# First scores on all 128 rows, with zero-padded copies of the queries, and no idle matmuls in the middle

## The chip, the core and the metric

The kernel runs on one core of a Trainium2 chip. The metric is the device time of one execution in microseconds (us); of several runs the median counts. The engines are PE (TensorE: matmuls, with PEld for its weight loads), DVE (VectorE), ACT (ScalarE), POOL (GpSimd) and SP (SyncE, which here issues DMAs). SBUF has 128 partitions. PSUM has 8 banks of 128 x 512 fp32; matmuls write there.

## The reference

Two attention layers over 2048 tokens of width 512, with 32 heads of 16, side by side in the output.

```python
def _A_ref(x, wqkv, wo):
    qkv = (x @ wqkv).reshape(B, S, 3, H, Dh).transpose(2, 0, 3, 1, 4)
    q, k, v = qkv[0], qkv[1], qkv[2]
    scores = jnp.einsum("bhqd,bhkd->bhqk", q, k) * Dh ** -0.5
    p = _softmax(scores, axis=-1)
    o = jnp.einsum("bhqk,bhkd->bhqd", p, v)
    return o.transpose(0, 2, 1, 3).reshape(B, S, D) @ wo

def _B_ref(x, wqkv, w_phi, wo):
    ...
    pq = jnp.einsum("bhsd,hdf->bhsf", q, w_phi)
    pk = jnp.einsum("bhsd,hdf->bhsf", k, w_phi)
    phi_q = concatenate([softmax(pq), softmax(-pq)], -1)
    phi_k = concatenate([softmax(pk), softmax(-pk)], -1)
    kv = jnp.einsum("bhsf,bhsd->bhfd", phi_k, v)
    z = jnp.einsum("bhsf->bhf", phi_k)
    num = jnp.einsum("bhqf,bhfd->bhqd", phi_q, kv)
    den = jnp.einsum("bhqf,bhf->bhq", phi_q, z)[..., None] + 1e-6
    return (num / den).transpose(0, 2, 1, 3).reshape(B, S, D) @ wo

return jnp.concatenate([a, b], axis=-1)
```

Layer A, full softmax attention, is nearly all of the work. Layer B, linear attention, runs in the gaps.

## The kernel before

Layer A is cut into 32 units. A unit is a group of four heads (`g`, eight groups) and a chunk of 512 queries (`c`, four chunks). Four heads of 16 are laid out at partitions 0, 32, 64 and 96: head r of a group has its 16 rows at 32r, followed by 16 rows which in the queries' tile are zero at first. `QT` holds the projected queries that way, `KT` the keys, whose rows 16 and 17 of each block are ones.

Each unit has two phases. In the first one the scores are computed with the queries as stationary operand (`emit_m1`, L716 to L728): 128 queries x 512 keys for one head per matmul, each on 32 rows of the array, at the tile position of its head. Two heads at a time fill two PSUM banks (0 and 1, or 2 and 3, alternately), and DVE takes the maximum over the keys (`emit_r1`, L735). After 32 such steps `emit_mchain` (L744 to L756) writes the negative maxima, in two bf16 parts, into rows 16 and 17 of the query blocks, by way of POOL, a DMA transpose and two DMAs. In the second phase (`emit_m2`, L771) the scores are computed again, transposed: 128 keys x 512 queries for one head, now with the maximum subtracted, since the keys' rows 16 and 17 are ones. ACT takes the exponential into one of the `RING` slots of `pT` (L782), and `emit_pv` (L796) multiplies it by the values plus a column of ones, four heads at a time, each on 17 columns of the array, all into bank 7. Banks 4, 5 and 6 go round among the second scores and the background pieces.

The order of work on each engine is written out by a planner: one loop over slots `tau`. In slot `tau` PE gets the two first-score matmuls of step `tau`, the two second-score matmuls of step `tau - LAG` (43 slots behind), every second slot the four matmuls of `emit_pv`, and then one background piece (`bg_step`) if one is due. Such a piece is mostly four full matmuls: projections of layer A (L321, L333), work of layer B (L452, L528, L634), the output projection (L661). If the slot has fewer than `NCOL = 2` columns of work after the scores, `emit_fill` (L823) adds idle matmuls: groups of four, each on 17 columns, a tile of ones times a tile of zeros, into bank 7, where they add zero. DVE gets the maximum of the slot, ACT the two exponentials and the copies out of PSUM.

PE executes in order. A first-score matmul of step `tau` waits for DVE's maximum of step `tau - 2`, which read the same banks. A second score waits until ACT has read the bank it takes.

Unit 0 takes its steps in another order than the rest, so that it can begin with the first keys. `u` counts units and `NQ` = 32 is the slots of a unit; the 1024 steps of first scores are followed by 46 slots in which the second phase runs out, and then by the last unit's end (`emit_last`).

SP issues its DMAs in order and waits in order as well: in a unit's course the copy of the sums out of `X` (`lr`, L834), their reciprocals to `Yd` (L846), four copies that spread these over 16 rows each (L849), and the two DMAs of the maxima for the second phase. POOL multiplies (L859) once the L849 copies have landed.

Layer B's feature maps use `uB` and `eB`, both double, one piece every 26 slots.

Of the kernel before, what the change touches and what calls it, by code (L numbers as in the profile page):

```python
# [94 lines left out]
def bass_concat_heads__softmax_full_mha__linear_kernel_hedgehog__prompt_kernel(  # L95
# [11 lines left out]
    NQ = 8 * NKC  # L107
    NB = 4 * NKT
    NU = NG * NQC
    RING = 16  # L110
    LAGX = 11
    PVLAG = 3
    RMLAG = 1
    NCOL = 2
# [3 lines left out]
    units = [(g, c) for c in range(NQC) for g in range(NG)]  # L118

    with contextlib.ExitStack() as es:  # L120
        block = es.enter_context(nc.Block())

        def sb(name, shape, dt):
            return es.enter_context(nc.sbuf_tensor(name, shape, dt))

        P = _Plan()
# [14 lines left out]
        PS = es.enter_context(nc.psum_tensor("PS", [128, 8, 512], F32))  # L141
# [13 lines left out]
        WKp = sb("WKp", [128, 4, NG, 128], BF)  # L155
        WOp = sb("WOp", [128, NG, 512], BF)
        QT = sb("QT", [128, NG, S], BF)
        KT = sb("KT", [128, NG, S], BF)
        VP = sb("VP", [128, NKT, H, 17], BF)
        pT = sb("pT", [128, RING, 512], BF)  # L160
        X = sb("X", [128, 2, 512], F32)
# [7 lines left out]
        woB = sb("woB", [128, 4, 512], BF)  # L169
        qmask = sb("qmask", [128, 4], F32)  # L170
        pB = sb("pB", [128, 2, 512], F32)
        uB = sb("uB", [128, 2, 1024], F32)
        eB = sb("eB", [128, 2, 1024], BF)
        sB = sb("sB", [128, 512], F32)
        mB = sb("mB", [128, 2, 2, 32], F32)
# [59 lines left out]
        t_stage0 = P.op("pool", lambda e: e.memset(flat(stage).bitcast(U32), 0), [t_wkp])  # L235
        t_bd0 = P.op("pool", lambda e: e.memset(flat(BD).bitcast(U32), 0))
        t_wo0 = P.op("pool", lambda e: e.memset(flat(WOp).bitcast(U32), 0))
        t_vp1 = P.op("pool", lambda e: e.memset(VP[:, :, :, 16:17], 1.0))
        t_yd1 = P.op("pool", lambda e: e.memset(Yd[:], 1.0))
        t_vb1 = P.op("pool", lambda e: e.memset(vB[:], 1.0))  # L240
# [23 lines left out]
        def later(slot, fn):  # L264
            calls.setdefault(slot, []).append(fn)
# [47 lines left out]
        qt_ready = {}  # L313
        kt_ready = {}
# [98 lines left out]
        users = {}  # L413

        def use(key):
            return users.get(key, [])
# [21 lines left out]
        def fm(n):  # L438
            x, st = (1, n) if n < NKT else (0, n - NKT)
            i = n % 2  # L440
            cx = {}
# [5 lines left out]
            def p_fin(b, tok, tau):  # L447
# [9 lines left out]
            u4 = uB[:, i, :].rearrange("p (h s f) -> p h s f", s=2, f=16)  # L457
# [10 lines left out]
            def sub(tau):  # L468
                def mb(k):
                    return mB[:, i, k, :].unsqueeze(2).broadcast_to([128, H, 16])  # L470
                P.op("pool", lambda e: e.tensor_tensor(u4[:, :, 0, :], p3, mb(0), ALU.subtract),  # L471
                     [cx["mx"]] + use(("u", i)))
                cx["u"] = P.op("pool", lambda e: e.tensor_tensor(u4[:, :, 1, :], mb(1), p3, ALU.subtract), [cx["mn"]])
                users[("p", i)] = [cx["u"]]
                users[("m", i)] = [cx["u"]]
                later(tau + 5, lambda: ex(tau + 5))

            def ex(tau):
                cx["e"] = P.op("act", lambda e: e.activation(eB[:, i, :], uB[:, i, :], ACT.Exp),  # L479
                               [cx["u"]] + use(("e", i)))  # L480
                users[("u", i)] = [cx["e"]]
                s = pool_slot(tau + 2)
                later(s, lambda: sums(s))

# [161 lines left out]
        for n in range(2 * NKT):  # L646
            fm(n)
# [28 lines left out]
        d_sh = [dsem("sh0"), dsem("sh1")]  # L676
        d_mt = [dsem("mt0"), dsem("mt1")]
        d_mr = [dsem("mr0"), dsem("mr1")]
        PVB = PS[:, 7, :]

        r1 = {}
# [18 lines left out]
        total_q1 = NU * NQ  # L700
# [14 lines left out]
        def emit_m1(q1):  # L715
            u, qt, kc, half = decode_q1(q1)  # L716
            g, c = units[u]
            q0 = c * 512 + qt * 128
            deps = [qt_ready[(g, c)], kt_ready[(g, kc)], r1.get(q1 - 2)]
            tok = None  # L720
            for i in range(2):
                r = 2 * half + i
                tok = P.op("pe", lambda e, r=r: e.matmul(  # L723
                    PS[:, r, :], QT[32 * r:32 * r + 32, g, q0:q0 + 128],
                    KT[32 * r:32 * r + 32, g, kc * 512:(kc + 1) * 512],
                    start=True, stop=True, tile_position=(32 * r, 0)), deps, signal=(i == 1))
                deps = []
            m1[q1] = tok  # L728

        def emit_r1(q1):  # L730
            u, qt, kc, half = decode_q1(q1)
# [47 lines left out]
        def emit_exp(B):  # L779
            slot = B % RING  # L780
            bank = bank_of[B]
# [5 lines left out]
        def emit_pv(u, kt):  # L787
# [6 lines left out]
            for B in Bs:  # L794
                r = block_info(B)[2]
                tok = P.op("pe", lambda e, B=B, r=r: e.matmul(  # L796
                    PVB[32 * r:32 * r + 17, :], VP[:, kt, 4 * g + r, :], pT[:, B % RING, :],
                    start=(kt == 0), stop=(kt == NKT - 1), tile_position=(0, 32 * r)),
# [9 lines left out]
            for B in Bs:  # L808
                slot_reader[B % RING] = tok
            pv_t[(u, kt)] = tok  # L810
# [68 lines left out]
        def emit_last():  # L879
# [21 lines left out]
            for k in range(4):  # L901
# [8 lines left out]
                else:  # L910
                    t = P.op("dve", lambda e, k=k, bank=bank: e.tensor_copy(ou[:, k, :], PS[:, bank, :]), deps)
                P.dma("sp" if k % 2 == 0 else "act", d_last[k], lambda e, st=st, k=k: e.dma_start(
                    out[0][st * 128:(st + 1) * 128, 0:512], ou[:, k, :]), [t])

        tau = 0
        while tau <= max(pv_in_slot) or jobs or running or calls:
            if tau < total_q1:
                emit_m1(tau)
            Pg = tau - LAG
            blocks = [2 * Pg, 2 * Pg + 1] if 0 <= Pg < total_q1 else []  # L920
            for B in blocks:
                emit_m2(B)
            for B in blocks:
                emit_exp(B)
            for fn in calls.pop(tau, []):
                fn()
            ncol = 0
            for (u, kt) in pv_in_slot.get(tau, []):
                emit_pv(u, kt)
                ncol += 1  # L930
                if u == NU - 1:
                    ncol += 1
                if kt == NKT - 1 and u == NU - 1:
# [69 lines left out]
```

## Time and profile before

| | us |
|---|---|
| median of 3 runs | 1341.0 |
| lowest, highest | 1339.66, 1344.04 |
| span of the profiled execution | 3156.6 |
| PE busy in it | 3152.2 |
| DVE busy in it | 1304.1 |
| ACT busy in it | 1296.2 |
| POOL busy in it | 307.0 |

The span of the profiled execution, from its first to its last instruction, is longer than the timed runs by more than a factor of two. No time is given for the profiled execution beside its span.

A row of a group reads: line, engine, operation, output<-inputs, shape, number | busy us, mean ns of one | idle time of the engine just before them and what ended it. A row of the timeline reads: start, duration, engine, line, operation. The ends of matmuls are modelled, so intervals between starts say more than durations. In a row of the stretches come the window, its length, and then busy time and number for PE, PEld, DVE, ACT and POOL, the granted clock of PE, and the share and rate of the DMAs.

### The profile page before, as it was taken

What the parts mean: (1) busy time and instruction counts of PE and PEld (TensorE: products, weight loads), DVE (VectorE), ACT (ScalarE), POOL (GpSimd) and SP (SyncE); (2) the same over time, 40 slices, a digit from 0 to 9 for tenths busy, and PEclk for the clock granted to TensorE, in tenths of its full rate; (3) what the DMA queues carried; (4) which work ended last, traced back from release to release, by engine and by line L of the source; (5) the groups of instructions that cost most, each with busy time, mean ns of one, the idle gap of its engine ahead of it and who ended that gap; (6) DMA issues with size and microseconds to landing.
All of it is one profiled execution on the core that took longest, in us unless ns stands there. A gap on an engine that the chain in (4) does not pass through costs nothing.

```text
span 3156.6 us, 29062 instructions
## 1 busy us (share of the span) xinstructions
PE 3152.2 (100%) x12226; PEld 362.2 (11%) x12226; DVE 1304.1 (41%) x1130; ACT 1296.2 (41%) x2479; POOL 307.0 (10%) x423
## 2 busy tenths in 40 slices
PE   9999999999999999999999999999999999999999
PEld 1111001111111111110011111111111111111111
DVE  1222223444444544544454435444454444445410
ACT  0001223444444444444444435444444444444442
POOL 1000000000011111111111101111111111111100
DMA  2000001000000000000000000000000000100000
GB/s 53 0 0 24 0 11 18 8 2 3 2 2 3 3 6 6 3 3 3 3 3 3 3 8 7 11 11 10 13 10 11 10 16 11 13 10 10 11 5 7
DMA packets 68939, 26.66 MB, mean 8 GB/s; under 512 B 59656, under 2 KB 66824, under 8 KB 68808
## 3 DMA queue, kind: packets, MB, share of 16 engines
q1 hardware_dynamic: 67464, 23.49, 5.4%
q8 instruction: 96, 1.57, 0.2%
q10 hardware_dynamic: 1344, 1.31, 0.1%
q14 instruction: 35, 0.29, 0.0%
HBM read 3.16 MB, written 4.19 MB: 2 GB/s over the span
## 4 chain that ended last, share of the span: by engine, by line
PE 99%; issue 0%; ACT 0%; POOL 0%; DVE 0%; POOLq 0%
PE PS L823 35%; PE PS L723 28%; PE PS L796 11%; PE PS L333 8%; PE PS L452 3%; PE PS L321 3%; PE PS L661 3%; PE PS L528 2%; PE PS L634 2%; PE PS L771 2%; PE PS L369 1%; PE PS L874 1%; PE PS L804 1%; PE PS L589 0%; PE PS L541 0%
## 5 line engine op out<-in xcount | busy, mean ns | idle before, releaser
L735 DVE TENSOR_REDUCE part<-PS 128x2 f32<-128x1024 f32 x1024 | 1255.2, 1226 | 1676.9 <-PE PS L723 1007.5
L782 ACT ACTIVATE pT<-PS 128x512 bf16<-128x512 f32 x2048 | 1111.5, 594 | 1262.1 <-PE PS L771 663.9
L823 PE MATMUL PS<-zmv,ones_t 128*17 128x512 bf16 x5004 | 1217.8, 973 | 0.3 <-ACT pT L782 0.3
L723 PE MATMUL PS<-KT,QT 32*128 32x512 bf16 x2048 | 959.5, 931 | 0.8 <-DVE QT L341 0.8
L771 PE MATMUL PS<-QT,KT 32*128 32x512 bf16 x2048 | 932.2, 902 | 0.0
L796 PE MATMUL PS<-pT,VP 128*17 128x512 bf16 x2048 | 457.2, 782 | 0.0
L723 PEld LDWEIGHTS PS<-KT,QT 32*128 32x128 bf16 x2048 | 111.0, 101 | 1580.8 <-DVE part L735 1102.9
L333 PE MATMUL PS<-xAT,WKp 128*128 128x512 bf16 x128 | 151.8, 1446 | 0.0
L823 PEld LDWEIGHTS PS<-zmv,ones_t 128*17 128x17 bf16 x5004 | 88.9, 88 | 315.1 <-issue 298.6
L771 PEld LDWEIGHTS PS<-QT,KT 32*128 32x128 bf16 x2048 | 111.1, 101 | 64.9 <-ACT pT L782 51.5
L333 PE MATMUL PS<-xAT,WQp 128*128 128x512 bf16 x128 | 116.5, 1122 | 0.0
L748 POOL TENSOR_SCALAR stage<-mrow 128x16 bf16<-128x16 f32 x32 | 8.1, 253 | 1070.4 <-DVE mrow L744 1070.4
L452 PE MATMUL PS<-WKp,xBT 128*128 128x512 bf16 x128 | 106.8, 1051 | 0.0
L345 ACT ACTIVATE KT<-PS,bias_k 128x512 bf16<-128x512 f32 x32 | 22.0, 687 | 194.9 <-PE PS L333 194.9
L507 POOL TENSOR_TENSOR wA<-eB,rB 128x1024 bf16<-128x1024 bf16 x32 | 61.7, 1929 | 398.1 <-ACT rB L501 398.1
L796 PEld LDWEIGHTS PS<-pT,VP 128*17 128x17 bf16 x2048 | 49.6, 87 | 378.0 <-issue 356.3
L321 PE MATMUL PS<-wA,xAT 128*128 128x512 bf16 x64 | 84.3, 1598 | 0.0
L859 POOL TENSOR_TENSOR QT<-X,Yd 128x256 bf16<-128x256 f32 x62 | 43.6, 725 | 400.6 <-DMA Yd<-Yd 400.4
L661 PE MATMUL PS<-WOp,QT 128*128 128x512 bf16 x96 | 80.8, 1063 | 0.0
L486 POOL TENSOR_TENSOR sB<-eB 128x512 f32<-128x512 bf16 x32 | 36.9, 1154 | 374.5 <-ACT eB L479 374.5
L471 POOL TENSOR_TENSOR uB<-pB,mB 128x512 f32<-128x512 f32 x32 | 33.9, 1058 | 395.9 <-DVE mB L462 395.9
L309 ACT ACTIVATE QT<-PS 128x512 bf16<-128x512 f32 x31 | 18.5, 597 | 93.7 <-PE PS L333 93.7
(78 smaller groups left out, 713.8 us busy)
## 6 DMA issues: line engine op xcount, KB each, us to landing
Yd<-Yd SPq DMA_DIRECT2D x124, 32.0 KB, 3.2
out_dram<-xAT SPq DMA_DIRECT2D x16, 128.0 KB, 1.7
out_dram<-OA SPq DMA_DIRECT2D x12, 128.0 KB, 1.7
wA<-in_A_wqkv_dram ACTq DMA_DIRECT2D x2, 512.0 KB, 5.0
QT<-mcols SPq DMA_DIRECT2D x64, 4.0 KB
wA<-in_A_wqkv_dram SPq DMA_DIRECT2D x1, 512.0 KB, 4.3
WOp<-in_A_wo_dram SPq DMA_DIRECT2D x4, 128.0 KB, 4.4
BD<-in_B_w_phi_dram SPq DMA_DIRECT2D x32, 0.5 KB, 1.6
```

The source lines that it names most:

```text
L321: piece = mm_piece(4, lambda e, b, ct: e.matmul(PS[:, b, :], xAT[:, ct, kt * 128:(kt + 1) * 128], wA[:, ct, 1024:1536], start=(ct == 0), s ...
L333: piece = mm_piece(4, lambda e, b, ct: e.matmul(PS[:, b, :], wpad[:, ct, g, :], xAT[:, ct, c * 512:(c + 1) * 512], start=(ct == 0), stop=( ...
L452: add_job(slot, [mm_piece(4, lambda e, b, ct: e.matmul(PS[:, b, :], xBT[:, ct, st * 128:(st + 1) * 128], Wf[:, x, ct, :], start=(ct == 0), ...
L528: piece = mm_piece(4, lambda e, b, ct: e.matmul(PS[:, b, :], xBT[:, ct, st * 128:(st + 1) * 128], wA[:, ct, 0:512], start=(ct == 0), stop= ...
L634: piece = mm_piece(4, lambda e, b, t: e.matmul(PS[:, b, :], oTB[:, i, t, :], woB[:, t, :], start=(t == 0), stop=(t == 3)), lambda: [cx["ot ...
L661: return mm_piece(4, lambda e, b, i: e.matmul(PS[:, b, :], QT[:, 4 * p + i, st * 128:(st + 1) * 128], WOp[:, 4 * p + i, :], start=(p == 0 ...
L723: tok = P.op("pe", lambda e, r=r: e.matmul(PS[:, r, :], QT[32 * r:32 * r + 32, g, q0:q0 + 128], KT[32 * r:32 * r + 32, g, kc * 512:(kc + 1 ...
L735: r1[q1] = P.op("dve", lambda e: e.tensor_reduce(part[:, u % 2, 2 * half:2 * half + 2, qt, kc], PS[:, 2 * half:2 * half + 2, :], AX.X, ALU ...
L771: m2_t[B] = P.op("pe", lambda e: e.matmul(PS[:, bank, :], KT[32 * r:32 * r + 32, g, kt * 128:(kt + 1) * 128], QT[32 * r:32 * r + 32, g, c ...
L782: exp_t[B] = P.op("act", lambda e: e.activation(pT[:, slot, :], PS[:, bank, :], ACT.Exp, scale=0.25), [m2_t[B], slot_reader.get(slot)])
L796: tok = P.op("pe", lambda e, B=B, r=r: e.matmul(PVB[32 * r:32 * r + 17, :], VP[:, kt, 4 * g + r, :], pT[:, B % RING, :], start=(kt == 0), ...
L823: P.op("pe", lambda e, cq=cq: e.matmul(PS[32 * cq:32 * cq + 17, bank, :], ones_t[:, 0:17], zmv[:, :], start=(bank != 7), stop=(bank != 7), ...
```

## The change

Five things are changed.

- A new tile `Q4` holds, for two units in turn, four copies of a unit's queries: copy r has the 16 rows of head r and zeros in all others. POOL zeroes it once at the start; four DMAs on SP (`emit_q4`) fill the 16 rows of each copy, 14 slots ahead of the unit (8 ahead of unit 1).
- From unit 1 on, a first score is one matmul on all 128 rows: stationary operand 128 queries out of `Q4`, moving operand 512 keys with all four heads. The zeros take the other heads out. Unit 0 keeps its form.
- `emit_fill` is called only in the first 32 slots and in the slots after the last first score.
- `RING`, the number of slots for exponentials, goes from 16 to 12.
- `uB` goes from two buffers to one.

```diff
-    RING = 16
+    RING = 12
...
+        Q4 = sb("Q4", [128, 2, 4, 512], BF)
...
-        uB = sb("uB", [128, 2, 1024], F32)
+        uB = sb("uB", [128, 1, 1024], F32)
...
         t_wo0 = P.op("pool", lambda e: e.memset(flat(WOp).bitcast(U32), 0))
+        t_q40 = P.op("pool", lambda e: e.memset(Q4[:].rearrange("p a b c -> p (a b c)").bitcast(U32), 0))
...
+        d_q4 = [dsem("q40"), dsem("q41")]
+        q4_t = {}
+        last_m1 = {}
+
+        def emit_q4(u):
+            g, c = units[u]
+            ub = u % 2
+            for r in range(4):
+                q4_t[u] = P.dma("sp", d_q4[ub], lambda e, r=r: e.dma_start(
+                    Q4[32 * r:32 * r + 16, ub, r, :], QT[32 * r:32 * r + 16, g, c * 512:(c + 1) * 512]),
+                    [qt_ready[(g, c)], t_q40, last_m1.get(u - 2)])
...
-            deps = [qt_ready[(g, c)], kt_ready[(g, kc)], r1.get(q1 - 2)]
+            deps = [kt_ready[(g, kc)], r1.get(q1 - 2)] + [qt_ready[(g, c)] if u == 0 else q4_t[u]]
...
-                tok = P.op("pe", lambda e, r=r: e.matmul(
-                    PS[:, r, :], QT[32 * r:32 * r + 32, g, q0:q0 + 128],
-                    KT[32 * r:32 * r + 32, g, kc * 512:(kc + 1) * 512],
-                    start=True, stop=True, tile_position=(32 * r, 0)), deps, signal=(i == 1))
+                if u == 0:
+                    tok = P.op("pe", lambda e, r=r: e.matmul(
+                        PS[:, r, :], QT[32 * r:32 * r + 32, g, q0:q0 + 128],
+                        KT[32 * r:32 * r + 32, g, kc * 512:(kc + 1) * 512],
+                        start=True, stop=True, tile_position=(32 * r, 0)), deps, signal=(i == 1))
+                else:
+                    tok = P.op("pe", lambda e, r=r: e.matmul(
+                        PS[:, r, :], Q4[:, u % 2, r, qt * 128:(qt + 1) * 128],
+                        KT[:, g, kc * 512:(kc + 1) * 512], start=True, stop=True), deps, signal=(i == 1))
                 deps = []
             m1[q1] = tok
+            last_m1[u] = tok
...
+        for u in range(1, NU):
+            later(u * NQ - 14 if u > 1 else NQ - 8, lambda u=u: emit_q4(u))
...
-            if ncol < NCOL:
+            if ncol < (NCOL if tau < NQ or tau >= total_q1 else 0):
                 emit_fill(NCOL - ncol)
```

In the changed file the first scores from unit 1 on stand at L742, the second scores at L790, the idle matmuls at L842, the copies at L689.

More of the change, by code (lines that the diff above doesn't have):

```diff
@@ L456, in fm @@
             p3 = pB[:, i, :].rearrange("p (h f) -> p h f", f=16)
-            u4 = uB[:, i, :].rearrange("p (h s f) -> p h s f", s=2, f=16)
+            u4 = uB[:, 0, :].rearrange("p (h s f) -> p h s f", s=2, f=16)
             e3 = eB[:, i, :].rearrange("p (g f) -> p g f", f=16)
@@ L471, in sub @@
                 P.op("pool", lambda e: e.tensor_tensor(u4[:, :, 0, :], p3, mb(0), ALU.subtract),
-                     [cx["mx"]] + use(("u", i)))
+                     [cx["mx"]] + use(("u", 0)))
                 cx["u"] = P.op("pool", lambda e: e.tensor_tensor(u4[:, :, 1, :], mb(1), p3, ALU.subtract), [cx["mn"]])
@@ L478, in ex @@
             def ex(tau):
-                cx["e"] = P.op("act", lambda e: e.activation(eB[:, i, :], uB[:, i, :], ACT.Exp),
+                cx["e"] = P.op("act", lambda e: e.activation(eB[:, i, :], uB[:, 0, :], ACT.Exp),
                                [cx["u"]] + use(("e", i)))
-                users[("u", i)] = [cx["e"]]
+                users[("u", 0)] = [cx["e"]]
                 s = pool_slot(tau + 2)
```

## The prediction

> **What bounds the kernel now.** I read the page's head and busy shares first, then the costliest groups, the stretches before and after 490 us, and last the timeline of single slots. A slot is one turn of the planner's loop: two first-score matmuls with one maximum on DVE, and two second-score matmuls with two exponentials on ACT.
>
> ```profile
> span 3156.6 us, 29062 instructions
> PE 3152.2 (100%) x12226; PEld 362.2 (11%) x12226; DVE 1304.1 (41%) x1130; ACT 1296.2 (41%) x2479; POOL 307.0 (10%) x423
> ...
> L735 DVE TENSOR_REDUCE part<-PS 128x2 f32<-128x1024 f32 x1024 | 1255.2, 1226 | 1676.9 <-PE PS L723 1007.5
> L823 PE MATMUL PS<-zmv,ones_t 128*17 128x512 bf16 x5004 | 1217.8, 973 | 0.3 <-ACT pT L782 0.3
> L723 PE MATMUL PS<-KT,QT 32*128 32x512 bf16 x2048 | 959.5, 931 | 0.8 <-DVE QT L341 0.8
> ```
>
> The profiled execution lasted 3156.6 us; the three timed runs have a median of 1341.0. The profile took 2.35 times as long, and PE was busy in all of it. So it is no picture of a timed run: DVE's 1304 us and ACT's 1296 us fill 41% of the profile, but nearly all of a timed run. Only PE's pace can differ that much, and the timeline shows how.
>
> ```profile
> 487.38 1.54 PE L723 MATMUL PS<-KT,QT 32*128 32x512 bf16 x2
> 487.39 1.33 PE L771 MATMUL PS<-QT,KT 32*128 32x512 bf16 x2
> 488.85 0.95 PE L796 MATMUL PS<-pT,VP 128*17 128x512 bf16 x4
> ...
> 562.09 0.91 PE L723 MATMUL PS<-KT,QT 32*128 32x512 bf16 x2
> 562.09 0.74 PE L771 MATMUL PS<-QT,KT 32*128 32x512 bf16 x2
> 562.92 0.76 PE L796 MATMUL PS<-pT,VP 128*17 128x512 bf16 x4
> 563.03 1.23 DVE L735 TENSOR_REDUCE part<-PS 128x2 f32<-128x1024 f32 x1 [1.29 <-PE PS L723]
> 563.61 3.43 PE L333 MATMUL PS<-xAT,WKp 128*128 128x512 bf16 x4
> ...
> 490.00:3015.00 2525.00, 2524.35 (x10936) 286.37 (x10932) 1193.06 (x1034) 1171.51 (x2256) 294.87 (x395) 1.00 0.06 7
> ```
>
> I call 512 columns streamed once through the array a pass. Two L723 and two L771, each on 32 of the 128 rows, start together at 562.09 and the next work starts at 562.92: four matmuls, one pass of 0.83 us. Four matmuls on 17 columns (L796, L823) are also one pass, a full matmul (L333, four in 3.43) is one by itself. At 487 us a pass still took 1.47. The granted clock stands at 1.00 in the stretch of slow passes too, so that column doesn't explain the pace.
>
> Passes before: 726 full ones (672 in the groups quoted with the background pieces below, 54 at the start and the end), 42 from small matmuls, 528 for L796 and L804, 5004/4 = 1251 idle ones (L823), 1067 shared by L723 and L771 (1024 slots and 43 tail slots). Sum 3614; times 0.84 is 3036, and the slow start brings it to 3152. The profiled execution is PE-bound. In a timed run a pass cannot exceed 1341/3614 = 0.371 us. From the other side:
>
> ```profile
> 1617.24 0.28 PE L541 MATMUL PS<-vB,wA 128*128 128x68 bf16 x2
> ...
> 1617.24 0.31 PE L541 MATMUL PS<-vB,wA 128*128 128x68 bf16 x3
> ```
>
> A third 68-column matmul ended 0.03 us after the second, 0.44 ns a column, an estimate of 0.226 for 512. So a timed pass lies between 0.226 and 0.371. I take 0.24, near the lower end, because the next sum needs no slow PE.
>
> ```profile
> 747.84 1.23 DVE L735 TENSOR_REDUCE part<-PS 128x2 f32<-128x1024 f32 x1 [2.98 <-PE PS L723]
> 748.98 0.67 DVE L462 TENSOR_REDUCE mB<-pB 128x32 f32<-128x512 f32 x1
> 749.57 0.67 DVE L464 TENSOR_REDUCE mB<-pB 128x32 f32<-128x512 f32 x1
> 750.20 1.23 DVE L735 TENSOR_REDUCE part<-PS 128x2 f32<-128x1024 f32 x1
> ...
> 7.14 0.69 DVE L230 COPY WKp<-wA 128x2048 bf16<-128x2048 bf16 x1 [1.34 <-DMA wA<-in_A_wqkv_dram]
> ...
> 3138.18 1.08 ACT L782 ACTIVATE pT<-PS 128x512 bf16<-128x512 f32 x2 [1.44 <-PE PS L771]
> ```
>
> Back to back, DVE starts its next work 1.14 us after a maximum (747.84 to 748.98), and a pair of L462 and L464 takes 1.22. DVE's floor is 1024 x 1.14 + 32 x 1.22 + 32 x 0.13 (L744, estimated) = 1210. Ahead of it lie the weight copy (7.83), eight passes and a copy, about 12 us. After it come 86 exponentials, at 1.08 - 0.59 = 0.49 each 42 us, and some 7 for the last products. Floor: 1271. The timed run is 70 us over it. DVE and ACT feed each other through one PE queue, with one spare pair of banks for DVE and three single banks for ACT, and I put the 70 us to that.
>
> **The change part by part.** Idle matmuls: 264 of 5004 stay, so 1185 passes go. First scores: from unit 1 on, 1984 matmuls take a pass each where L723 rode along with L771 for nothing; 11 slots had no L771, so 1973 are added. Net +788 passes, 4402 in all. Against the profile's own time that is 788 x 0.84 = +662, so 3819 at the profile's pace. This is what the profile of the changed kernel should show if PE is held back in the same way.
>
> In a timed run the passes lie under DVE's work until one slot has too many.
>
> ```profile
> 41.30 0.69 DVE L341 CAST QT<-PS 128x512 bf16<-128x512 f32 x1 [33.47 <-PE PS L333]
> 42.05 0.09 PEld L723 LDWEIGHTS PS<-KT,QT 32*128 32x128 bf16 x2 [3.40 <-DVE QT L341]
> ```
>
> From DVE's end (41.99) to PE's start: 0.06. From a pass's end (562.92, when the next begins) to DVE's start (563.03): 0.11. Count from the maximum that frees a pair of banks. The maximum of the slot after next can start at 2 x 1.14 = 2.28, if its scores are there. In a slot with a background piece of four full passes, PE before does 1 + 4 passes, and 1 more in every second slot for L796: at 0.24, 0.06 + 6 x 0.24 + 0.24 + 0.11 = 1.85, in time. After, it does 2 + 1 + 4, or 8: 0.06 + 8 x 0.24 + 0.48 + 0.11 = 2.57, late by 0.29; with 7 passes 2.33, late by 0.05. Mean 0.17. Such pieces come four matmuls at a time:
>
> ```profile
> L333 PE MATMUL PS<-xAT,WKp 128*128 128x512 bf16 x128 | 151.8, 1446 | 0.0
> L333 PE MATMUL PS<-xAT,WQp 128*128 128x512 bf16 x128 | 116.5, 1122 | 0.0
> L452 PE MATMUL PS<-WKp,xBT 128*128 128x512 bf16 x128 | 106.8, 1051 | 0.0
> L321 PE MATMUL PS<-wA,xAT 128*128 128x512 bf16 x64 | 84.3, 1598 | 0.0
> L661 PE MATMUL PS<-WOp,QT 128*128 128x512 bf16 x96 | 80.8, 1063 | 0.0
> L634 PE MATMUL PS<-woB,xAT 128*128 128x512 bf16 x64 | 53.1, 1039 | 0.0
> ```
>
> With L528 (64, as L634) these are 672 matmuls, 168 groups, less 2 ahead of the loop and 26 in the first 32 slots, which keep the old form: 140. So 140 x 0.17 = 24 us. At 0.226 it is 11, at 0.27 it is 64. A plain slot has 3 or 4 passes, at most 0.96, and fits. What is late next is the second-score pair, one queue place behind, and its exponentials; ACT takes 2 x 0.49 of 1.18 and catches up.
>
> The copies: 124 DMAs on SP, four per unit.
>
> ```profile
> Yd<-Yd SPq DMA_DIRECT2D x124, 32.0 KB, 3.2
> ...
> 1316.15 2.47 SPq L849 DMA_DIRECT2D Yd<-Yd x4
> ...
> L237 POOL MEMSET WOp<- 128x2048 uint32 x1 | 1.8, 1805 | 0.0
> ...
> POOL QT L859 <- DMA Yd<-Yd: 400.4, 20, 95.8
> ```
>
> The nearest row is as many small SBUF copies: 2.47 to issue four, 3.2 to land, 5.7 together. They are issued 14 slots ahead, at 1.2 us each 17, so first scores don't wait; before unit 1, 8 slots are 9.6. Their other conditions (the projected queries, and the last scores two units back) are met long before. Queued behind them on SP is the copy of the reciprocals, one slot later, then the four L849 copies, which L859 on POOL awaits 7 slots after. That wait may grow by up to 2.5 us. The products are read only after eight units, and what is behind on POOL (the feature maps' sums) has 5 slots until ACT asks. I cost it at nothing; uncovered it would be 31 x 2.5 = 77 us. No gain is possible here: nothing is taken from SP.
>
> Q4's zeros are as large as WOp's, 1.8 us on POOL before VP's ones. These were done 12.3 us into the profile, so at 14.1; in a timed run the first V copy could wait up to 1.8 us on ACT, where exponentials haven't begun. Nothing, at most 1.8. Twelve slots: an exponential waits for the product that read its slot, which PE issued two slots before the second score that it waits for anyway. Nothing. One uB: its pieces come 26 slots apart. Nothing.
>
> Sum: 1341 + 24 = 1365.
>
> **Rivals.** *A, faster: the idle matmuls stood in the way.* When ACT is late, PE waits in front of a second score, and the next first scores come behind everything queued there. Before, that was 1 + 2 + 1 = 4 passes, always; after, 1 + (0 or 1) + 2 = 3.5. Half a pass of 0.24 in some 840 plain slots is 101 us, more than the whole gap of 70 over DVE's floor. For it: a 70 us gap whose cause no row shows. Against it: PE has about 0.4 us to spare in a plain slot. If half the gap goes: 1306.
>
> *B, slower and PE-bound.* From 4402 x p = 1341, thus p = 0.305, PE sets the pace in every slot from unit 1 on. At 0.34 it gives 1497. For it: the profile shows PE held back without a trace in the clock column, and 0.34 contradicts nothing before: there the fullest slots would be late by 0.27, or 140 x 0.135 = 19 of the 70. Against it: the three timings agree within 0.4%, which suits DVE better than a clock that wanders.
>
> The Trainium skill, "TensorE: Matmul & The Clock Gate", Part 1, says that the array runs at half its clock after a window without work and at full clock when busy, 427 ns a pass at the slow rate. By that an idler PE would be a slower one, and 4402 passes would give an estimate of 1880. The trace disagrees: its passes are 0.84 and 1.47 with PE busy throughout.
>
> As a mechanism from rows alone: PE works 3 passes of a slot before, 3 to 4 after, so leaving out idle matmuls makes it no idler. I give a drop of the pace by idleness 0.04, inside B.
>
> *C, no change.* The late slots are absorbed by what ACT costs anyway: 1341.
>
> **How the numbers follow.** Forecast 0.36, own range 1352 to 1405 (0.226 and 0.27 a pass); A 0.33; B 0.21; C 0.10. A difference under 0.3% can't be told from none. Faster 0.33, same 0.10, slower 0.57. The range runs from 1300, just under A, to 1480, B at 0.336.
>
> **What would show it.** In the profile after: about 4400 passes; L742's two matmuls a pass apart instead of together; no wait of PE on Q4's copies except at a unit's start; the DVE's waits behind slots with background pieces. If PE is held back as before, a span near 3800. The forecast is wrong if plain slots change as much as those with pieces (A or B), or if DVE waits at the first slot of each unit (the copies).

## The result, and the profile after

| | before | after |
|---|---|---|
| median (us) | 1341.36 | 1417.93 |
| lowest, highest | 1339.66, 1344.04 | 1415.02, 1422.14 |
| after to before, 95% interval | | 1.0575 [1.0553, 1.0597] |

The changed kernel is slower by 77 us; 24 were forecast. To see where they went, a profile of before at the pace of its timed runs is needed, since the one ahead of the prediction was taken with PE held back. It was taken again (experiment 1, span 1344.4) and stands for "before" from here on. First the page's head of after: span, busy times, granted clock in 40 slices, and the chain that ended last by engine.

```profile
span 1416.2 us, 19606 instructions
PE 1324.6 (94%) x7351; PEld 383.6 (27%) x7486; DVE 1233.0 (87%) x1130; ACT 1235.6 (87%) x2479; POOL 308.4 (22%) x424
PEclk9999999999999999999999999999999999999999
PE 65%; DVE 15%; ACT 14%; DMA 3%; issue 2%; SPq 1%; POOL 0%; ACTq 0%; POOLq 0%
```

The same lines of before:

```profile
span 1344.4 us, 29062 instructions
PE 1211.9 (90%) x12226; PEld 342.5 (25%) x12226; DVE 1225.6 (91%) x1130; ACT 1214.9 (90%) x2479; POOL 306.8 (23%) x423
PEclk9999999999999999999999989998898999889899
DVE 37%; ACT 30%; PE 27%; DMA 3%; SPq 1%; issue 1%; POOL 0%; ACTq 0%
```

The chain has moved from DVE and ACT to PE: 27% of it before, 65% after. DVE's work is the same, 1226 and 1233 us, in a span 72 us longer. So DVE idles more. The groups of after that tell of waits (busy, mean of one | idle before, and what ended most of it):

```profile
L754 DVE TENSOR_REDUCE part<-PS 128x2 f32<-128x1024 f32 x1024 | 1188.4, 1221 | 123.7 <-PE PS L742 120.8
L790 PEld LDWEIGHTS PS<-QT,KT 32*128 32x128 bf16 x2048 | 132.6, 91 | 507.9 <-ACT pT L801 283.6
L742 PEld LDWEIGHTS PS<-KT,Q 128*128 128x128 bf16 x1984 | 125.7, 98 | 244.4 <-DVE part L754 115.5
```

And of before, whose maxima stand at L735, second scores at L771 and first scores at L723:

```profile
L735 DVE TENSOR_REDUCE part<-PS 128x2 f32<-128x1024 f32 x1024 | 1181.3, 1220 | 60.2 <-PE PS L771 55.6
L771 PEld LDWEIGHTS PS<-QT,KT 32*128 32x128 bf16 x2048 | 152.4, 91 | 107.7 <-ACT pT L782 79.4
L723 PEld LDWEIGHTS PS<-KT,QT 32*128 32x128 bf16 x2048 | 96.3, 91 | 506.4 <-DVE part L735 360.7
```

DVE's idle time ahead of the maxima has doubled (60 to 124). By these rows the weight loads of first scores wait for DVE less than before (116 us, not 361): PE comes to its first scores late. That those of second scores idle 284 us until ACT, not 79, is not PE waiting for ACT, as two loads of after show:

```profile
703.33 0.09 PEld L790 LDWEIGHTS PS<-QT,KT 32*128 32x128 bf16 x2 [0.42 <-ACT pT L801]
...
704.18 0.30 PEld L790 LDWEIGHTS PS<-QT,KT 32*128 32x128 bf16 x2 [0.42 <-issue]
```

The weight loads stand idle for 0.42 us in both slots, whether ACT is named or nothing, and the matmuls stand equally far behind their first scores, 0.54, in both (timeline below). A real wait for ACT shows in the starts of a slot's two second scores: either they start together, or the second one starts 0.05 us after the end of an instruction on ACT. By a count over the traces these delays add up to 143 us before and 105 after. They have not grown.

Why PE is late, a timeline of plain slots shows. After (start, duration, engine, line):

```profile
702.47 0.39 PE L815 MATMUL PS<-pT,VP 128*17 128x512 bf16 x4
...
702.79 0.60 PE L742 MATMUL PS<-KT,Q 128*128 128x512 bf16 x2
...
703.33 0.39 PE L790 MATMUL PS<-QT,KT 32*128 32x512 bf16 x2
...
703.65 0.61 PE L742 MATMUL PS<-KT,Q 128*128 128x512 bf16 x2
...
704.19 0.60 PE L790 MATMUL PS<-QT,KT 32*128 32x512 bf16 x2
```

Before:

```profile
704.17 0.39 PE L723 MATMUL PS<-KT,QT 32*128 32x512 bf16 x2 [0.20 <-DVE part L735]
...
704.50 0.39 PE L796 MATMUL PS<-pT,VP 128*17 128x512 bf16 x4
...
704.72 0.39 PE L823 MATMUL PS<-zmv,ones_t 128*17 128x512 bf16 x4
...
705.30 0.39 PE L723 MATMUL PS<-KT,QT 32*128 32x512 bf16 x2 [0.20 <-DVE part L735]
```

From L796 to L823, both on 17 columns, 0.22 us pass; from L723 and L771 (32 rows) to L796 it is 0.33. After, L790 to L742 and L815 to L742 take 0.32, two L742 and the step to L790 0.54. The median over all such pairs of these traces is 0.216 between matmuls of one kind and 0.312 to 0.318 where the kind changes (full rows, 32-row tiles, 17-column tiles). So a pass costs 0.22 and a change of kind another 0.10. The Trainium skill, "TensorEngine Tiling (Array Packing)", Key Properties, says that a change of tiling mode drains the array, and gives no figure; these rows agree and give one.

By these medians PE's work in two plain slots, one with a product and one without, is before 2 x (0.315 + 0.212 + 0.312) = 1.68 us, idle matmuls included, and after (0.216 + 0.312 + 0.317) + (0.216 + 0.312 + 0.315 + 0.316) = 2.00. DVE needs 1.13 per maximum (704.17 to 705.30 above), 2.26 for two. What PE has to spare fell from 0.58 to 0.26. The slot with the product takes 1.16 of the 2.00 and is by itself longer than 1.13. In many such slots the second of the second scores also starts late for its bank, as at 704.19, where the duration of 0.60 holds two starts 0.21 apart. So the medians over plain slots of after, from the last first score of one slot to that of the next, are 0.86 without a product and 1.39 with one, 2.25 together: of DVE's 2.26 nothing is left.

One slot with a background piece in the timeline of after:

```profile
249.56 0.38 PE L790 MATMUL PS<-QT,KT 32*128 32x512 bf16 x1 [0.47 <-ACT pT L801]
...
250.20 0.60 PE L742 MATMUL PS<-KT,Q 128*128 128x512 bf16 x2
...
250.74 0.39 PE L790 MATMUL PS<-QT,KT 32*128 32x512 bf16 x2
250.84 1.23 DVE L754 TENSOR_REDUCE part<-PS 128x2 f32<-128x1024 f32 x1 [0.52 <-PE PS L742]
...
251.06 1.04 PE L335 MATMUL PS<-xAT,WQp 128*128 128x512 bf16 x4
...
251.93 0.59 PE L742 MATMUL PS<-KT,Q 128*128 128x512 bf16 x2
...
252.56 2.41 DVE L754 TENSOR_REDUCE part<-PS 128x2 f32<-128x1024 f32 x2 [0.50 <-PE PS L742]
```

DVE idles 0.52 already ahead of the piece, since a second score of the plain slot before it had waited for ACT (at 249.56). With the piece PE takes 1.73 from first scores to first scores (250.20 to 251.93), 0.60 more than DVE's 1.13, and DVE idles 0.50 again.

I put each idle time of DVE ahead of a maximum to what PE did between that maximum's first scores and those before (a count over the trace, gaps over 0.04 us, counted from the pace of 1.13 and so 0.09 longer each than in the rows above, where a maximum lasts 1.22). Behind slots with background work it is 53 us before and 110 after, behind plain slots 24 and 37. Together +70, of a span longer by 72. The 139 pieces of four full matmuls from unit 1 on have 44 us of it before and 97 after.

### The profile page after: what moved, and what is told of

The parts are those of the page before. It is cut to its first block, busy times and chain, and to the rows that moved or that the text cites. A ratio compares the mean times of both kernels' runs of the same rounds, so it can differ in the third digit from the quotient of the medians.

```text
span 1416.2 us, 19606 instructions
## 1 busy us (share of the span) xinstructions
PE 1324.6 (94%) x7351; PEld 383.6 (27%) x7486; DVE 1233.0 (87%) x1130; ACT 1235.6 (87%) x2479; POOL 308.4 (22%) x424
## 4 chain that ended last, share of the span: by engine, by line
PE 65%; DVE 15%; ACT 14%; DMA 3%; issue 2%; SPq 1%; POOL 0%; ACTq 0%; POOLq 0%
PE PS L742 23%; PE PS L790 19%; DVE part L754 13%; ACT pT L801 10%; PE PS L815 8%; PE PS L335 4%; PE PS L454 2%; ACT eB L481 2%; PE PS L663 2%; PE PS L636 1%; DMA WQp<-wA 1%; PE PS L323 1%; PE PS L530 1%; DVE mB L464 1%; DMA xAT<-WQp 1%
## 5 line engine op out<-in xcount | busy, mean ns | idle before, releaser
L754 DVE TENSOR_REDUCE part<-PS 128x2 f32<-128x1024 f32 x1024 | 1188.4, 1221 | 123.7 <-PE PS L742 120.8
L742 PE MATMUL PS<-KT,Q 128*128 128x512 bf16 x1877 | 577.5, 385 | 40.3 <-DVE part L754 25.4
L790 PE MATMUL PS<-QT,KT 32*128 32x512 bf16 x2048 | 489.5, 386 | 14.9 <-ACT pT L801 11.9
L790 PEld LDWEIGHTS PS<-QT,KT 32*128 32x128 bf16 x2048 | 132.6, 91 | 507.9 <-ACT pT L801 283.6
L815 PE MATMUL PS<-pT,VP 128*17 128x512 bf16 x2048 | 202.1, 385 | 15.7 <-ACT X L311 15.5
L742 PEld LDWEIGHTS PS<-KT,Q 128*128 128x128 bf16 x1984 | 125.7, 98 | 244.4 <-DVE part L754 115.5
L815 PEld LDWEIGHTS PS<-pT,VP 128*17 128x17 bf16 x2048 | 49.4, 87 | 134.0 <-issue 109.4
L491 POOL TENSOR_TENSOR sB<-sB 128x256 f32<-128x256 f32 x64 | 36.0, 562 | 5.0
L481 ACT ACTIVATE eB<-uB 128x1024 bf16<-128x1024 f32 x32 | 34.2, 1069 | 0.0
L335 PE MATMUL PS<-xAT,WQp 128*128 128x512 bf16 x123 | 32.5, 381 | 0.7 <-issue 0.3
L454 PE MATMUL PS<-WKp,xBT 128*128 128x512 bf16 x120 | 32.1, 381 | 0.8 <-issue 0.6
L335 PE MATMUL PS<-xAT,WKp 128*128 128x512 bf16 x124 | 32.2, 381 | 0.7 <-issue 0.6
```

The source lines that it names most:

```text
L335: piece = mm_piece(4, lambda e, b, ct: e.matmul(PS[:, b, :], wpad[:, ct, g, :], xAT[:, ct, c * 512:(c + 1) * 512], start=(ct == 0), stop=( ...
L454: add_job(slot, [mm_piece(4, lambda e, b, ct: e.matmul(PS[:, b, :], xBT[:, ct, st * 128:(st + 1) * 128], Wf[:, x, ct, :], start=(ct == 0), ...
L491: t = P.op("pool", lambda e, w=w: e.tensor_tensor(s3[:, :, 0:w], s3[:, :, 0:w], s3[:, :, w:2 * w], ALU.add), [t])
L742: tok = P.op("pe", lambda e, r=r: e.matmul(PS[:, r, :], Q4[:, u % 2, r, qt * 128:(qt + 1) * 128], KT[:, g, kc * 512:(kc + 1) * 512], start ...
L754: r1[q1] = P.op("dve", lambda e: e.tensor_reduce(part[:, u % 2, 2 * half:2 * half + 2, qt, kc], PS[:, 2 * half:2 * half + 2, :], AX.X, ALU ...
L790: m2_t[B] = P.op("pe", lambda e: e.matmul(PS[:, bank, :], KT[32 * r:32 * r + 32, g, kt * 128:(kt + 1) * 128], QT[32 * r:32 * r + 32, g, c ...
```

## The experiments

"Before" and "after" name the kernel from which an edit starts; ratios are to the kernel before.

**1. Before, once more**, for a profile at its timed pace (shown above).

> The kernel before, unchanged, for a profile at the pace of the timed runs. Theory Q (the new first scores fill PE's queue: a pass more in each slot, and 0.10 us more at each change between kinds of matmuls, as 702.47 to 702.79 in the changed kernel's trace shows; idle matmuls and copies cost nothing): a span near 1340, a pass of 0.22 us, DVE idle for about 70 us between its maxima, against 147 in the changed kernel. If the profile is again held back, the span is near 3157 and only its time counts.

It took 1346.2 us. DVE idles 77 us in it; the prediction's floor had left 70.

**2. Idle matmuls left out alone.** Before, with the change's condition:

```diff
-            if ncol < NCOL:
+            if ncol < (NCOL if tau < NQ or tau >= total_q1 else 0):
```

> The kernel before without the idle matmuls of the middle, nothing else changed. Theory Q: they lie in DVE's shadow, 1336 to 1346 us. Rival A (the idle matmuls stood in the way): 1306, at most 1325. Rival G (the idle matmuls hold PE's clock up): over 1400, with a granted clock under 0.95 in the middle.

1474.7 us, ratio 1.0987 [1.0956, 1.1017]. The page's granted clock says why:

```profile
PEclk9975678977568555555566755555555865555579
```

Mean 0.664. The idle matmuls hold PE's clock; without them it falls although PE has the same work otherwise. The Trainium skill, "TensorE: Matmul & The Clock Gate", Part 1, says that activity releases a throttle of half rate, which is the default; here the clock was 0.62 from 340 to 1200 us while PE's busy share was 88%, so that share doesn't tell whether PE counts as busy.

**3. Full-row first scores alone.** After, with the idle matmuls of before (the diff above turned round).

> The changed kernel with the idle matmuls of the middle put back. Theory Q: a plain slot gets 0.54 + 0.32 + 0.32 + 0.22 = 1.40 us of PE work, over DVE's 1.13, so some 840 plain slots cost 0.25 to 0.27 more each: about 1640 us. Rival A: the loss of the changed kernel isn't PE's queue, the idle matmuls cost about what it says they cost before, 35 us: about 1455. Rival R (the copies on SP cost the time): about 1418 to 1425.

1578.5 us, 1.1759 [1.1708, 1.1811], clock 1.000. From the page's head:

```profile
PE 1559.2 (99%) x12226; PEld 408.5 (26%) x12226; DVE 1292.8 (82%) x1130; ACT 1270.1 (81%) x2479; POOL 308.7 (20%) x424
```

This is the PE-bound case, somewhat under the time expected for it. Each half of the change alone makes the kernel slower by more than both together: full rows hold the clock in place of the idle matmuls, and leaving these out makes room for the passes.

**4. All but first scores and idle matmuls** (copies, zeros and waits of `Q4`, 12 slots, one `uB`). After, with experiment 3's edit and:

```diff
-                if u == 0:
+                if True:
```

> The changed kernel with the copies, their zeros, the waits on them, 12 exponential slots and one uB, but with the first scores of all units in the old form out of QT, and with the idle matmuls of before; the copies are not used. Theory Q: 1338 to 1348 us. Rival R (copies late, or SP's queue late for what stands behind them: reciprocals, transposes of the linear layer): 1375 to 1418.

1341.0 us, 0.9987 [0.9962, 1.0012]: they cost nothing.

**5 and 6. Background pieces halved**, after and before: a piece of four matmuls (those of layer A's values apart) becomes two pieces of two, in slots that follow each other.

```diff
+        def halves(n, fn, deps=()):
+            return [mm_piece(2, fn, deps), mm_piece(2, lambda e, b, i: fn(e, b, i + 2))]
...
-            piece = mm_piece(4, lambda e, b, ct: e.matmul(
+            piece = halves(4, lambda e, b, ct: e.matmul(
```

> The changed kernel with its background pieces of four matmuls cut into two pieces of two, in slots one after the other. Theory P (peaks: only slots with a piece are too long, 1.16 + 0.86 us and the next first scores 0.43 against 2.26): with two matmuls 1.16 + 0.43 + 0.43 + 0.17 = 2.19 fits, so most of DVE's 147 us of idle time goes that the kernel before doesn't have: 1345 to 1370. Theory L (load: two plain slots take PE 2.00 us of DVE's 2.26, so what is once late stays late, and the sum of PE's work is the same): 1400 to 1425. Rival K (a piece now holds one of three banks for two slots): over 1425.

> The kernel before with its background pieces cut in the same way. Theory P: 48 us of DVE's idle time come behind slots with a piece of four, half or more of it goes: 1305 to 1325. Theory L: two plain slots take PE 1.68 of 2.26, nothing is late for long: 1335 to 1345. Rival K (banks): 1350 or more; the slots of the halves have no idle matmuls, so the granted clock may fall under 0.97.

After: 1441.9, 1.0753 [1.0732, 1.0774]; before: 1352.9, 1.0093 [1.0073, 1.0112]. If only the peak of a slot counted, smaller peaks would have helped. They cost 24 us instead, as rival K had it. A piece now holds one of the three banks of the second scores for two slots, and the delays of second scores, counted as above, rise from 105 to 125 us in after and from 143 to 188 in before.

**7. Fewer changes of kind.** After, with second scores ahead of first scores in even slots, four changes in two slots instead of five.

```diff
+            if tau < total_q1 and (tau % 2 == 1 or not blocks):
+                emit_m1(tau)
             for B in blocks:
                 emit_m2(B)
+            if tau < total_q1 and not (tau % 2 == 1 or not blocks):
+                emit_m1(tau)
```

> The changed kernel with the second scores ahead of the first ones in slots without a product, so that two slots have four changes between kinds of matmuls on PE instead of five. The same matmuls, 0.10 us less per two slots, some 50 us of PE's time. Theory L (load, the price of a change included): 1365 to 1395. Theory N (passes alone count, the changes cost nothing on the path): 1412 to 1424. Above that if first scores behind a second score that waits for ACT are what counts.

1478.6, 1.1031 [1.1010, 1.1052]. The change saved is there, but two pairs of second scores now follow each other with no first scores between them, and the later one waits for its bank, with both first-score pairs behind it:

```profile
700.45 0.81 PE L790 MATMUL PS<-QT,KT 32*128 32x512 bf16 x2
700.87 0.09 PEld L790 LDWEIGHTS PS<-QT,KT 32*128 32x128 bf16 x1 [0.34 <-ACT pT L801]
...
701.19 1.04 PE L742 MATMUL PS<-KT,Q 128*128 128x512 bf16 x4
```

The delays of second scores rise from 105 to 206 us. In this queue a wait weighs more than 0.10 us of changing.

**8. Full rows in every second step.** After, with `if u == 0 or half == 1:` for the old form.

> The changed kernel with the full-row first scores in every second slot only (banks 0 and 1); the others are in the old form and share a pass with the second scores. Half of the added passes, and three changes of kind in two slots instead of five: 0.54 + 0.32 + 0.22 + 0.32 = 1.40 us of PE work in two slots, less than before the change (1.68). Theory L with the clock held: 1335 to 1355. Rival G (the work left doesn't hold the clock): a granted clock under 0.85 and 1380 to 1450.

1661.7, 1.2401 [1.2373, 1.2429], clock 0.743; it falls in the same way as in experiment 2, to 0.67 from 800 us on. Half of the full-row passes don't hold the clock, as rival G had it, but the time is far above its 1450.

**9. The old form only behind background pieces** of four matmuls, about one slot in seven. After, with:

```diff
-                if u == 0:
+                if u == 0 or bg_before[0]:
...
-            ncol += bg_step(tau)
+            nbg = bg_step(tau)
+            ncol += nbg
+            bg_before[0] = nbg == NCOL
```

> The changed kernel, but the first scores of the slot that follows a background piece of four matmuls are in the old form (two 32-row matmuls that share a pass, and that are of one kind with the second scores), all others on full rows. About one slot in seven gets it. Theory L (too little of PE's time is left over two slots to make up what a slot with a piece loses): the slots with a piece lose one pass (0.216) and one change of kind (0.10) less, so DVE's idle time behind them falls from 110 us to about what the kernel before has there, 48, and the time is 1418 - 62 = 1356, down to 1345 if the idle time behind plain slots (36 us) goes with it. Rival (plain slots are short by themselves, through the wait for ACT in front of second scores, and pieces only start it): DVE's idle time behind plain slots stays at 36 or grows, and the time stays above 1385. Rival G (the clock needs every full-row pass): granted clock under 0.95 and over 1420.

1396.1, 1.0404 [1.0358, 1.0451], clock 0.989: 22 us better than after, not 62. DVE's groups, with what ended its idle time:

```profile
L755 DVE TENSOR_REDUCE part<-PS 128x2 f32<-128x1024 f32 x1024 | 1187.0, 1219 | 105.0 <-PE PS L791 64.7 <-PE PS L743 36.6 <-PE PS L738 0.6
```

First scores in the old form share their pass with second scores (L791), so most of what is left still lies behind pieces. By the count used above DVE's idle time behind slots with background work fell from 110 to 89 us, not to 48, and behind plain slots it stayed at 37. The saving was taken too high: from a piece of full-row matmuls to first scores on full rows the kind doesn't change, but to the old form it does. From last first scores to last first scores PE takes 1.61 us in a slot with a piece of four and no product, 1.72 in after; with a product it is 2.05 against 2.17. So 0.12 is saved, not 0.316, and the 21 us that DVE idles less are 0.14 for each of the 148 slots with first scores in the old form. The rival's numbers came true (37 and a time above 1385), but the saving that did come shows that what PE does in these slots counts.

**10. Fewer idle matmuls in before**: none in slots with a small piece of layer B (`cols=1` left out at two places).

> The kernel before, without the one group of idle matmuls that it adds in slots with a small background piece of layer B (the two kinds of piece that count as one column). DVE idles 28.6 us behind those slots in the kernel before, at 76 waits. If the idle group is what makes them late (0.216 and a change of kind of 0.10 against a mean wait of 0.38), most of the 28.6 goes: 1341 - 25 = 1316. Rival: these slots wait for ACT's copies or for POOL, not for PE's own work: 1336 to 1344. Rival G (every idle group holds the clock): some 128 of 1250 groups are gone, granted clock below 0.975 and over 1345.

1349.5, 1.0058 [1.0035, 1.0082], clock 0.959. A miss, and its ground was misread: of the 28.6 us, 24 lay behind plain slots with idle matmuls. Rival G came true: fewer idle matmuls, a lower clock and a longer time. No version that beats the kernel before was found.

**11 to 15. Loads taken off.** Three kernels leave out the product of exponentials and values for all but the first and last keys of a unit (11: after; 13: with experiment 9's edit as well; 15: before). 14 is a first form of 15 in which the idle matmuls fell into banks 4 to 6. 12 shortens the exponentials from 512 to 448 columns, in after and in before (`pT` is filled with ones at the start).

```diff
         def emit_pv(u, kt):
+            if u < NU - 1 and 0 < kt < NKT - 1:
+                return
```

```diff
-                pT[:, slot, :], PS[:, bank, :], ACT.Exp, scale=0.25), [m2_t[B], slot_reader.get(slot)])
+                pT[:, slot, 0:448], PS[:, bank, 0:448], ACT.Exp, scale=0.25), [m2_t[B], slot_reader.get(slot)])
```

*11:*

> The changed kernel, with the product of exponentials and values left out except for the first and the last keys of a unit (the last unit keeps all): the output isn't the reference's. Two plain slots of PE work fall from 2.00 us to 4 x 0.216 + 2 x 0.315 + ... = 1.69, what the kernel before has with its idle matmuls (1.68); slots with a piece and the queue's order stay. Theory L (what was lost is PE's time to spare over two slots): DVE's idle time falls from 147 to about the 77 of the kernel before, and the time is 1418 - 70 = 1348, between 1335 and 1360. Rival W (the second scores now come 0.53 us behind the first ones instead of beside them, and every wait for ACT or DVE in PE's queue delays the other engine as well): only the idle time behind slots with a product goes, 36 us, and the time stays at 1380 or above. Rival G: clock under 0.95 and over 1400.

1458.8, 1.0831 [1.0768, 1.0895], clock 0.887: with less work PE's clock falls again, so the whole time answers nothing. But until 340 us the clock is full in this kernel too, and the number of maxima that DVE gets done from 60 to 340 us can be compared. The expectations below quote the sum of two adjoining stretches, which counts a maximum on their border twice; the single stretch has one less. The rows give window, its length, DVE busy in maxima and their number, granted clock and the DMAs. Before, after, and after with few products:

```profile
60.00:340.00 280.00, 262.49 (x228) 1.00 0.12 18
```

```profile
60.00:340.00 280.00, 243.69 (x210) 1.00 0.13 20
```

```profile
60.00:340.00 280.00, 251.87 (x218) 1.00 0.13 20
```

The change loses 18 maxima of 228 there; taking 0.3 us of PE's work off two plain slots, which brings it to before's, gives 8 back. Slots with a piece and a product are lighter by it too. Experiment 9 gives 5 (215).

*12:*

> The changed kernel, with the exponentials taken over 448 of the 512 queries (the rest of their slots is filled with ones at the start, so the output isn't the reference's). An exponential takes about 64 columns x 0.8 ns, some 0.05 us, less than its 0.52 from start to start: 2048 x 0.05 = 105 us less work on ACT. Rival W (PE waits for ACT in front of second scores, and first scores stand behind it): PE's waits for ACT in front of second scores fall from 284 us to under half, DVE's idle time falls below 90, and the time to 1340 to 1365. Theory L (PE's own passes are what is late): DVE's idle time stays above 120, and the time above 1390.

> The kernel before with the same shorter exponentials, to see what they are worth where PE has time to spare. If its 70 us over DVE's floor are waits for ACT: 1341 - 50 = 1290 or less. If they are DVE's idle time behind slots with a piece: 1330 to 1342. Theory L wants the gap between the two kernels to stay near 77 with shorter exponentials; rival W wants it to shrink below 45.

After: 1390.8, 1.0352 [1.0315, 1.0389]; before: 1325.1, 0.9853 [0.9813, 0.9892]. An exponential is 0.06 us shorter, and the delays of second scores fall from 105 to 71 us in after and from 143 to 93 in before. DVE's idle time in after, 122 us by the count above, and the time lie just within what theory L wanted. The gap between the kernels is 66 us instead of 77, nearer to theory L than to rival W's 45: ACT's time has a part in the loss, a small one. The before kernel fell between its two expected ranges.

*13, and the controls 14 and 15:*

> The changed kernel with both reliefs at once: few products (as above, output not the reference's) and first scores in the old form behind background pieces. Read between 60 and 340 us, where the clock is 1.00 in all of these kernels: DVE does 229 maxima there in the kernel before, 211 in the changed one, 216 with the old form behind pieces, 219 with few products. Theory L (PE's passes and changes of kind, in plain slots and behind pieces, are all of the loss): 226 to 230. Theory M (the place of the second scores, a first-score pair later than before, costs by itself): at most 223. The whole time is not read, as the clock falls later.

> The control for it: the kernel before with few products (output not the reference's; the idle matmuls are not added in their place). Between 60 and 340 us. If PE has time to spare there already, as theory L has it: 227 to 232 maxima while the clock is 1.00. If fewer waits in PE's queue help by themselves: 235 or more.

> The control once more, since in the first one the idle matmuls fell into banks 4 to 6 and waited there for ACT: the kernel before with few products (output not the reference's), and its idle matmuls in bank 7 as ever. Between 60 and 340 us, with the clock at 1.00: 227 to 232 maxima if PE has time to spare in the kernel before (theory L), so that 223 with both reliefs leaves a rest of about six maxima unexplained by PE's load; 222 to 225 if few products cost as much by themselves, so that the two reliefs explain all of it.

From 60 to 340 us, both loads off, and the control without the fault, each in one execution:

```profile
60.00:340.00 280.00, 257.44 (x223) 1.00 0.13 20
```

```profile
60.00:340.00 280.00, 264.63 (x230) 1.00 0.12 19
```

The spoilt control had 223, since its idle matmuls waited for ACT. The two loads together give back 13 of the 18 to 20 maxima lost, the sum of 8 and 5. A rest of 7 against the control stays: 223 is what theory M wanted. But it doesn't show that the place of the second scores costs by itself, for not all of PE's load is off: in 13 the slots with a piece still have their own first scores on full rows. It is there that DVE idles more. In these 280 us it is 20.6 us behind slots with background work, against 13.6 in before, 11.2 in the control and 34.0 in after; behind plain slots 2.2, 4.0, 3.3 and 4.6. And the delays of second scores are shorter in 13, 98 us in the whole run against 182 in the control.

## Why the prediction was right and where it was wrong

*Direction and mechanism.* Slower, and by PE's passes in a slot becoming too many for DVE's pace, as forecast. 1417.93 lies above the forecast's own range, 1352 to 1405, and inside the whole one only because that reached to 1480 for a rival that fell. The pass at full clock, taken as 0.24 within 0.226 to 0.371, measured 0.216, just under the lower bound. The first scores stand a pass apart instead of together (702.79 to 703.33 above holds two passes and a change), no row shows PE waiting for the copies, and most of DVE's idle time lies behind background pieces.

*The step that failed* is the term "Mean 0.17 ... 140 x 0.17 = 24 us", with its sequel, "A plain slot has 3 or 4 passes, at most 0.96, and fits. What is late next is the second-score pair ... and catches up". Behind the 139 pieces of four DVE lost 53 us more, 0.38 each; behind smaller pieces 4 and in plain slots 13, all of that in slots with a product (17 to 36; without one it falls, from 7 to 1). Three things were wrong in the sum:
- It lets PE start 0.06 us after the maximum that frees the banks, and so counts 1.85 of 2.28 as in time before and only what goes beyond 2.28 as lost after. But PE mostly comes later. By a count over the traces the first scores of slots with a piece of four start 0.42 us after that maximum on average before, and 0.46 after, and before idles 44 us behind the pieces itself. With little lead to use up, most of what PE takes beyond one maximum of DVE is lost. In after PE takes 1.72 us (2.17 with a product) from last first scores to last first scores at the median, 0.59 and 1.04 more than 1.13, and DVE idles 0.51 and 0.81 behind such slots on average, stretches at half clock left out. In experiment 9 PE takes 0.12 less there, and DVE's idle time falls by about as much.
- A change of kind had no price. With 0.216 a pass and 0.10 a change the same sum gives a lateness of 0.05 or 0.36, a mean of 0.20 and 140 x 0.20 = 28 us: higher, and still little more than half. A plain slot with a product doesn't fit either: 1.16 against 1.13.
- ACT doesn't simply catch up. A second score that waits for ACT's bank holds the next first scores in PE's queue. These delays are no longer than before (105 and 143 us), but before they fell into time that PE had to spare, and after there is none. Making them longer, as experiments 5 and 7 do, costs 24 and 61 us over after; making them shorter, as experiment 12 does, gains 27.

That PE has so little lead at a piece because its plain slots leave no time for one is read from medians of one trace; no kernel tried it alone. Taking load off PE gave back 13 of the 18 to 20 maxima lost, with part of the load still on.

*Edits costed at nothing.* Right: copies, zeros, 12 slots and one `uB` together, 0.9987.

*Rival A* (idle matmuls in the way, 1306) falls: without them alone, 1.0987, though at a lower clock. *Rival B* (PE-bound, from 0.305 a pass) falls with the pass of 0.216. The drop of pace by idleness, given 0.04 inside B, is real, but not in the changed kernel: "leaving out idle matmuls makes it no idler" held, at a clock of 0.993, only because the full-row scores came with it. A falling clock decides experiments 2 and 8 and not this change; that PE had been busy throughout in the slow execution was no evidence against it. Why that execution was slow, with passes 3.9 times 0.216, no run shows. *Rival C* (no change) falls. A span near 3800 was for a PE held back, and it wasn't.

## What to carry to other kernels

Sum an in-order engine's work over a whole period of the schedule, changes of tiling included, and set it against the pace of the engine it feeds: where the ordinary slots leave no time to spare, a heavier slot finds little lead, and most of its excess is lost. Check in a trace whether the engine really stands waiting where a sum starts it. An idle time with another engine's name behind it may be no wait for that engine; the distance between starts tells. Work that computes nothing may be what holds a clock, so test leaving it out by itself before counting it as a gain. Where two consumers are fed by one queue, a wait for one of them delays the other, and order and banks can matter more than the number of instructions.

## What the hardware showed that was not expected

- The granted clock depends on what PE does in a way that its busy share doesn't show: 0.976 with idle matmuls (PE 90% busy), 0.664 without (89%), 0.743 with full rows in every second step (88%), 0.993 with full rows in every step (94%).
- The idle matmuls don't quite hold it either: the runs of the kernel before go from 1335.7 us at a clock of 0.988 to 1350.1 at 0.970.
- It falls late as well as early: with few products it was 1.00 until 340 us and 0.87 from 400 to 1200.
- Taking work off PE can thus cost time: few products made the changed kernel slower, 1458.8 against 1417.9.
- A change between full rows, 32-row tiles and 17-column tiles costs 0.10 us, nearly half a pass of 512 columns.
